# Local attention and FFT convolution on one core: filter spectrum and sine tables moved into batch 0's attention, crossbar transposes for batches 2 and 3, early casts by the DMA

## The chip, the cores and the metric

The kernel runs on one core of a Trainium2 chip. Times are device microseconds (us) of one execution, as a median over runs. The profile is one execution recorded by the hardware profiler. PE is TensorE (the matmul engine), DVE VectorE, ACT ScalarE, POOL GpSimd; SP only issues DMAs here. Each of PE, DVE, ACT and POOL has its own queue of instructions in the order of the program, and in the traces here one whose data is late holds up those behind it (experiment 4 has PE standing 4.3 us so). An eviction is the copy of a matmul's result out of PSUM. A crossbar transpose is a DMA that transposes on its way (`dma_start_transpose`). A run is called slow when it is over 1.5% above the fastest of the same kernel; ratios leave slow runs out.

## The reference

Four batches of 8-head attention (768 positions, head size 64), each query seeing 8 global keys and the 96 last keys with an ALiBi bias, followed by a gated FFT convolution ("Hyena") and an output projection:

```python
scores = scale * np.matmul(q, k.transpose(0, 1, 3, 2)) + bias      # bias = -slope[h] * dist
a = softmax(np.where(is_global | is_local, scores, -1e9))
x = np.matmul(a, v).transpose(0, 2, 1, 3).reshape(4, 768, 512)
proj = x @ w_proj
x1, x2, x3 = proj[..., :D], proj[..., D:2*D], proj[..., 2*D:]
H = np.fft.rfft(filter_fft, n=S, axis=0)
y = x1 * np.fft.irfft(np.fft.rfft(x2, n=S, axis=1) * H, n=S, axis=1) * x3
return y @ w_out
```

The kernel does the FFTs as matmuls with sine tables that it computes itself. "Filter stage" is everything that depends on `filter_fft` and the tables: angles, sines, the filter's spectrum (`h1`, `h2`), and the inverse tables (transposes of the forward ones). A "gate" is one block of the product `x1 * x3` with its two projections; it needs no FFT and no table.

## The kernel before

Python generators emit small chunks of work; `weave` merges several generators into the one order in which every engine gets its instructions. A stream `(gen, n, a, b)` spreads its n chunks evenly over the part a to b of a stretch. Nothing is reordered afterwards: the position in this order decides what an engine waits behind.

```python
def emit(self):
    ...
    self.weave((self.attention(*qkv, *x, first=cast), 33, 0, 1))     # attention of batch 0, alone
    self.load_more_weights()                                         # gate weights
    loads = [qkv, self.load_batch(1)]
    self.load_w_out()
    for b in range(self.B):
        streams = [(self.hyena(b, *x, early=(b == 0)), 30, 0, 1)]    # early: 8 gates ahead of the FFT
        nx = None
        if b == 0:
            streams.insert(0, (self.filter_stage(), 16, 0.0, 0.4))
        ...
        if b + 1 < self.B:
            nx = self.new_x()
            streams.insert(0, (self.attention(*loads[b + 1], *nx), 33,
                               0.4 if b == 0 else 0.0, 0.95))
        self.weave(*streams)
        x = nx

def filter_stage(self):                       # angles by PE and ACT, folded by DVE, sines by ACT
    self.fwd = self.cp.tile([P, 3, 6, P], F16)
    ths = []
    for a in range(4):
        ths.append(self.dft_angles(a))
        for k in range(2):
            self.after(k + 1, lambda k=k, a=a: self.dft_fold(k, *ths[a]))
        yield 1
    ...
    for a in range(4):
        self.dft_sines(a, ths[a][0])
    yield from self.filter_spectrum()
    yield from self.inverse_tables()

def transpose_q(self, hp, qt, first):         # q and k of each head pair are transposed by PE
    ...
    for st in range(6):
        nc.tensor.transpose(tq[:, P * st:P * st + P], src[:, st], self.ident)
    ... nc.vector.tensor_copy(QT, tq[:, 0:S])
```

The five stretches of the program, in time: attention of batch 0; Hyena 0 with the filter stage and attention 1; Hyena 1 with attention 2; Hyena 2 with attention 3; Hyena 3.

The softmax here doesn't subtract the row's maximum and nothing guards it: scores larger than these inputs give would overflow.

Of the kernel before, what the change touches and what calls it, by code (L numbers as in the profile page):

```python
# [23 lines left out]
X1_SCALE = 64.0  # L24

# [19 lines left out]
class Fused:  # L45
# [45 lines left out]
    def batch_tiles(self):  # L91
        D = self.D
        qt = self.ld.tile([P, 6, self.H, D], F16, tag="q")
        kt = self.ld.tile([P, 7, self.H, D], F16, tag="k")
        vt = self.ld.tile([P, 7, self.H, D + 1], F16, tag="v")
        self.nc.gpsimd.memset(vt[:, :, :, D:D + 1], 1.0)  # L96
        return qt, kt, vt

    def load_tiles(self, dst, src, b):

        g, D = self.nc.gpsimd, self.D
        for t in range(7):
            lo = max(0, self.K0[t] - NG)
            hi = self.K0[t] + KL
            g.dma_start(dst[P - (hi - lo):P, t, :, 0:D],  # L105
                        src[b, :, lo:hi, :].rearrange("h p d -> p h d"))
            if t == 0:
                g.dma_start(dst[0:NG, 0, :, 0:D],
                            src[b, :, 0:NG, :].rearrange("h p d -> p h d"))
        if b > 0:  # L110
            self.nc.sync.dma_start(dst[0:NG, 1:7], dst[0:NG, 0:1].to_broadcast(
                [NG, 6] + list(dst.shape[2:])))

    def load_batch(self, b):
        g = self.nc.gpsimd
        qt, kt, vt = self.batch_tiles()
        for t in range(6):
            g.dma_start(qt[:, t], self.q[b, :, P * t:P * t + P, :].rearrange("h p d -> p h d"))  # L118
        self.load_tiles(kt, self.k, b)
        self.load_tiles(vt, self.v, b)  # L120
        return qt, kt, vt

    def load_first(self):


        nc, D = self.nc, self.D
        self.first = []
        for hp in range(4):
            hs = slice(2 * hp, 2 * hp + 2)
            for eng, src in ((nc.sync, self.q), (nc.sync, self.k)):  # L130
                st = self.stage([P, 2, 6, D])
                eng.dma_start(st.rearrange("p h r d -> p h (r d)"),
                              src[0, hs].rearrange("h (p r) d -> p h (r d)", r=6))
                self.first.append(st)

    def cast_first(self, hp):
        sq, sk = self.first[2 * hp:2 * hp + 2]
        out = []
        pool = self.nc.gpsimd.tensor_copy
        for cp, src in ((pool if hp > 1 else self.nc.vector.tensor_copy, sq),  # L140
                        (pool if hp > 1 else self.nc.scalar.copy, sk)):
            t = self.mp.tile([P, 6, P], F16, tag=f"c{len(out)}", name="t")
            cp(t.rearrange("p t (h d) -> p t h d", h=2), src.rearrange("p h t d -> p t h d"))
# [3 lines left out]
    def stage(self, shape):  # L147
        t = self.mp.tile([P, 768], F32, tag="stg", bufs=6)
# [8 lines left out]
    def load_weights(self):  # L157
        g, cp, DM = self.nc.gpsimd, self.cp, self.DM
        self.w = cp.tile([P, 4, 3 * DM], F16)
        self.wr = self.w_proj.rearrange("(t p) n -> p t n", p=P)  # L160
        g.dma_start(self.w[:, :, DM:2 * DM], self.wr[:, :, DM:2 * DM])
        self.fl = self.mp.tile([P, 6, DM], F16, tag="g", bufs=2)
        g.dma_start(self.fl, self.filt.rearrange("(t p) n -> p t n", p=P))

    def load_more_weights(self):
        for o in (0, 2 * self.DM):
            self.nc.gpsimd.dma_start(self.w[:, :, o:o + self.DM], self.wr[:, :, o:o + self.DM])
# [6 lines left out]
    def distances(self):  # L174
# [4 lines left out]
        for ap, w, first in ((dg, n, NG), (dm[:, 2, n - 48:n], 48, NG + o)):  # L179
            g.iota(ap, pattern=[[1, w]], base=first, channel_multiplier=-1,  # L180
                   allow_small_or_imprecise_dtypes=True)

            for sgn, off in ((1, 0), (-1, NL - 1)):
                if w == 48 and sgn < 0:
                    continue
                g.affine_select(ap, ap, pattern=[[sgn, w]], base=off + sgn * first,
                                channel_multiplier=-sgn, compare_op=Alu.is_ge, fill=HUGE)

        g.affine_select(dm[:, 2, n - 48:n], dm[:, 2, n - 48:n], pattern=[[0, 48]],
                        base=-NG - o, channel_multiplier=1, compare_op=Alu.is_ge, fill=HUGE)  # L190
# [3 lines left out]
        v.memset(dm[0:NG, :, 0:KL], float(NL))  # L194
        v.memset(dm[0:NG, :, KL:n], HUGE)
        v.memset(dm[0:NG, 2, n - 48:n], float(NL))
        d0 = dm[0:NG, 0, 0:KL]
        v.memset(d0, HUGE)
        for sgn, off in ((1, 0), (-1, NL - 1)):
            g.affine_select(d0, d0, pattern=[[sgn, KL]], base=off, channel_multiplier=-sgn,  # L200
                            compare_op=Alu.is_ge, fill=float(NL))
# [8 lines left out]
    def dft_rows(self):  # L210

        nc, sp = self.nc, self.sp
        i = self.mp.tile([1, 384], I32, tag="p2", name="i")
# [10 lines left out]
    def dft_angles(self, a):  # L224
# [26 lines left out]
        nc.scalar.activation(th, an, Act.Copy, bias=MAGIC, scale=1.0 / S)  # L251
        return th, an

    def dft_fold(self, k, th, an):
        if k == 0:
            self.nc.vector.tensor_scalar(th, th, MAGIC, -float(self.S), op0=Alu.subtract,
                                         op1=Alu.mult)
        else:
            self.nc.vector.tensor_add(th, th, an)
# [9 lines left out]
    def busy(self, n):  # L269


        if n:
            pt = self.mm()
# [3 lines left out]
    def inverse_tables(self):  # L277
# [3 lines left out]
        for sp in range(3):  # L281
            tp = self.ps.tile([P, 1024], F16, tag="tr", bufs=1)
# [4 lines left out]
            nc.vector.tensor_copy(self.inv[:, 2 * sp:2 * sp + 2].rearrange("p c r -> p (c r)"),  # L287
# [39 lines left out]
    def filter_stage(self):  # L327
        self.fwd = self.cp.tile([P, 3, 6, P], F16)
        ths = []
        for a in range(4):  # L330
            ths.append(self.dft_angles(a))
            for k in range(2):
                self.after(k + 1, lambda k=k, a=a: self.dft_fold(k, *ths[a]))
            yield 1
        yield 1
        yield 1
        for a in range(4):
            self.dft_sines(a, ths[a][0])
# [3 lines left out]
    def filter_spectrum(self):  # L342
# [4 lines left out]
        f2 = [self.mp.tile([P, 3, DM], F16, tag="stg", bufs=6, name="f2") for _ in range(2)]  # L347
# [5 lines left out]
        sc = 2.0 * H_SCALE  # L353

        def evac(s, pt):
            if s < 4 and s % 2 == 0:
                nc.scalar.mul(self.h1[:, s], pt, sc)
                nc.vector.tensor_scalar(self.h1[:, s + 1], pt, sc, None, op0=Alu.mult)
                if s == 0:
                    nc.scalar.mul(self.h1[0:1, 0], pt[0:1], H_SCALE)  # L360
            elif s < 4:
                nc.scalar.mul(self.h2[:, s - 1], pt, sc)
                nc.vector.tensor_scalar(self.h2[:, s], pt, -sc, None, op0=Alu.mult)
                if s == 1:
                    nc.scalar.mul(self.h1[0:1, 1], pt[0:1], H_SCALE)
                    nc.vector.memset(self.h2[0:1, 0:2, :], 0.0)
            else:
                nc.scalar.mul(self.h1[0:64, s], pt[0:64], sc)
                nc.scalar.mul(self.h1[64:P, s], pt[0:64], sc)
                nc.vector.tensor_scalar(self.h2[0:64, s], pt[64:P], sc, None, op0=Alu.mult)  # L370
                nc.vector.tensor_scalar(self.h2[64:P, s], pt[64:P], -sc, None, op0=Alu.mult)
        for s in range(6):
            self.forward(s, f2[0], f2[1], evac)
            yield 1


    def attention(self, qt, kt, vt, xT, xa, xb, first=None):
# [3 lines left out]
        qk, cst = {}, {}  # L381

        def trq(i):
            if i < n:
                qk.setdefault(i, {})[0] = self.transpose_q(i, cst[i][0] if first else qt, first)

        def trk(i):
            if i < n:
                qk.setdefault(i, {})[1] = self.transpose_k(i, cst[i][1] if first else kt, first)

        def sc(i, g):
            if i < n:
                self.weights(i, g, qk[i][0], qk[i][1])
                if first and g > 0 and i + 1 < n:
# [9 lines left out]
        def trx(i):  # L404
            self.transpose_x(i, xn.pop(i), xT)
# [9 lines left out]
        if first:  # L415
            cst[0] = first
        trq(0)
        yield 1
        cast(1)
        trk(0)  # L420
        yield 1
        for i in range(n + 1):
            if first and i == 1:
                self.nc.vector.tensor_copy(vt[0:NG, 1:7], vt[0:NG, 0:1].to_broadcast(
                    [NG, 6, self.H, self.D + 1]))
            for live, fn in ((i < n, lambda: sc(i, 0)),
                             (i + 2 < n and first, lambda: cast(i + 2)),
                             (i + 1 < n, lambda: trk(i + 1)),
                             (i < n, lambda: sc(i, 1)),
                             (i > 0, lambda: val(i - 1, 0)),  # L430
                             (i + 1 < n, lambda: trq(i + 1)),
                             (i > 0, lambda: val(i - 1, 1)),
                             (i < n, lambda: sc(i, 2)),
                             (i > 0, lambda: trx(i - 1))):
# [10 lines left out]

    def transpose_q(self, hp, qt, first):
        nc, S = self.nc, self.S
        hs = slice(2 * hp, 2 * hp + 2)
        QT = self.ap_.tile([P, S], F16, tag="qT")
        tq = self.ps.tile([P, 1024], F16, tag="tr", bufs=1)  # L450
        src = qt if first else qt[:, :, hs, :]
# [299 lines left out]
```

## Time and profile before

The prediction was made from 239.95 us (median of 3 runs).

| stretch | us | PE busy | ACT busy | DVE busy | granted clock |
|---|---|---|---|---|---|
| attention 0 | 45.2 | 31.4 | 21.8 | 30.3 | 0.89 |
| Hyena 0, filter, attention 1 | 73.4 | 56.8 | 43.6 | 50.0 | 0.88 |
| Hyena 1, attention 2 | 43.9 | 41.8 | 30.1 | 33.1 | 1.00 |
| Hyena 2, attention 3 | 43.9 | 41.7 | 30.0 | 33.1 | 1.00 |
| Hyena 3 | 34.2 | 28.9 | 18.9 | 14.7 | 1.00 |

It comes from the busy time by windows of the kernel before. Columns: window, its length, then busy us (and count of instructions) of PE, PE's weight loads, DVE, ACT and POOL, granted PE clock, DMA share and GB/s (the DMA share is the time of all packets over that of the 16 engines, and can pass 1):

```profile
0.00:45.20 45.20, 31.36 (x279) 16.96 (x280) 30.27 (x70) 21.78 (x29) 35.83 (x55) 0.89 2.01 191
45.20:118.60 73.40, 56.84 (x447) 30.28 (x446) 49.98 (x95) 43.57 (x69) 27.30 (x35) 0.88 1.10 65
118.60:162.50 43.90, 41.82 (x400) 23.54 (x398) 33.09 (x71) 30.10 (x51) 12.06 (x14) 1.00 1.27 100
162.50:206.40 43.90, 41.65 (x394) 23.29 (x392) 33.08 (x71) 30.04 (x50) 0.00 (x0) 1.00 0.10 37
206.40:240.60 34.20, 28.88 (x154) 14.71 (x152) 14.69 (x27) 18.94 (x35) 0.00 (x0) 1.00 0.18 67
```

Two steady stretches are 95% full on PE; the second stretch is 77% full, at a lower clock, and is the long one. The page's rows of busy tenths in 40 slices (6 us each, counted from 0) of the kernel before show where:

```profile
PE   4575968887978665867999999899999997999883
PEclk9998597997999995697999999999999999999999
DMA  6999999999991000002999910033000002400006
```

The DMA engines are full (9 tenths, by the packets' time) until slice 12 (72 us), and PE has its holes in slices 13 to 18 (78 to 114 us). The chain of waits of the kernel before (start, duration, what) shows what the second stretch waits for first:

```profile
53.07 1.28 ACT L267
54.36 2.40 ACT fwd L267 x4
...
57.24 0.51 ACT h_767 L357
57.77 0.70 DVE h_767 L358
58.49 0.59 ACT h_767 L360
59.08 0.49 ACT h_768 L362
59.59 0.70 DVE h_768 L363
60.31 0.59 ACT h_767 L365
```

L267 are the table load for Sin and the sines, L357 to L365 the filter's evictions, alternating between ACT and DVE. And one oddity of attention 0, from its timeline on DVE and on POOL:

```profile
15.46 3.52 DVE L506 TENSOR_TENSOR E_96<-E_96,mask 128x432 f16<-128x432 f16 x2
16.36 3.30 POOL L143 CAST t<-t 128x768 f16<-128x768 f32 x4
```

Two DVE multiplies that take 0.38 us each elsewhere (median of 32) took 3.52 us together while POOL casted.

### The profile page before, as it was taken

The numbers are of one execution on the slowest core, as the hardware profiler recorded it, in microseconds if no ns is written. First come the engines' busy times: TensorE is split into PE (matmuls) and PEld (weight loads), VectorE is DVE, ScalarE is ACT, GpSimd is POOL, SyncE is SP. The second block draws the span as 40 slices with busy tenths as digits, with TensorE's granted clock in tenths as the row PEclk, the third lists the DMA queues.
The fourth block names the chain that finished last, engine by engine and source line by source line (L and its number), as shares of the span: only waits on it lengthen the run. The fifth ranks groups of instructions, "written<-read, shape, count | busy, mean of one in ns | idle before, by whom it ended". The sixth has DMA issues, their size and how long they took to land.

```text
span 240.6 us, 4274 instructions
## 1 busy us (share of the span) xinstructions
PE 200.6 (83%) x1664; PEld 108.8 (45%) x1664; DVE 161.1 (67%) x334; ACT 144.4 (60%) x232; POOL 75.2 (31%) x102
## 2 busy tenths in 40 slices
PE   4575968887978665867999999899999997999883
PEld 1333545332445342544545565455556554455541
DVE  5587586683675896597246999943599994139550
ACT  4462574477553863573668748466866765774643
POOL 6969478987930000004977200000000000000000
PEclk9998597997999995697999999999999999999999
DMA  6999999999991000002999910033000002400006
GB/s 190 347 132 197 204 155 149 122 171 148 129 119 11 0 3 0 3 0 18 191 246 142 114 10 3 0 143 123 0 3 0 4 0 102 162 0 0 3 34 229
DMA packets 79572, 21.68 MB, mean 90 GB/s; under 512 B 71328, under 2 KB 76480, under 8 KB 79552
## 3 DMA queue, kind: packets, MB, share of 16 engines
q0 software_dynamic: 73584, 11.67, 86.1%
q1 hardware_dynamic: 5968, 9.74, 12.2%
q8 instruction: 13, 0.21, 0.4%
q14 instruction: 7, 0.06, 0.1%
HBM read 26.48 MB, written 6.29 MB: 136 GB/s over the span
## 4 chain that ended last, share of the span: by engine, by line
PE 47%; DVE 23%; ACT 10%; issue 3%; ACTq 0%; DVEq 0%
PE pt L552 9%; PE pt L566 9%; PE pt L649 8%; PE pt L631 5%; PE pt L323 4%; DVE g L557 3%; DVE xn L527 3%; PE sp L490 3%; ACT E_99 L497 3%; PE tx L534 2%; PE o L517 2%; PE o L522 1%; PE tk L478 1%; PE tq L453 1%; DVE X L592 1%
## 5 line engine op out<-in xcount | busy, mean ns | idle before, releaser
L552 PE MATMUL pt<-xT,w 128*128 128x384 f16 x256 | 47.8, 331 | 2.1 <-ACT x_861 L556 1.7
L552 PEld LDWEIGHTS <-w 128*128 128x128 f16 x256 | 24.1, 99 | 18.8 <-issue 4.4
L497 ACT ACTIVATE E_99<-sp 128x864 f16<-128x864 f32 x24 | 21.5, 897 | 13.4 <-PE sp L490 12.7
L649 PE MATMUL pt<-wo,y 128*128 128x512 f16 x96 | 24.4, 396 | 2.6 <-DVE y L642 2.6
L497 ACT ACTIVATE E_96<-sp 128x864 f16<-128x864 f32 x24 | 21.5, 894 | 7.7 <-PE sp L490 7.6
L105 POOL DMA_DIRECT2D vt<-in_v_dram x28 | 25.1, 911 | 2.6 <-DMA kt<-in_k_dram 1.2
L490 PE MATMUL sp<-QT,KT 64*128 64x216 f16 (+2 forms) x224 | 18.5, 258 | 6.4 <-ACT E_99 L497 2.6
L631 PE MATMUL pt<-inv,X 128*128 128x384 f16 x96 | 20.6, 351 | 3.7 <-DVE X L592 3.6
L652 ACT ACTIVATE t<-pt 128x512 f32<-128x512 f32 x24 | 14.3, 597 | 13.7 <-PE pt L649 13.6
L105 POOL DMA_DIRECT2D kt<-in_k_dram x21 | 18.9, 916 | 6.8 <-DMA qt<-in_q_dram 3.3
L527 DVE TENSOR_TENSOR xn<-o,rc 128x448 f16<-128x448 f32 x32 | 20.0, 625 | 1.1
L568 ACT CAST dst<-pt 128x512 f16<-128x512 f32 x24 | 14.1, 587 | 8.8 <-PE pt L566 8.8
L323 PE MATMUL pt<-dst,fwd 128*128 128x512 f16 x72 | 18.9, 380 | 0.0
L275 PE MATMUL pt<-idle 128*128 128x512 f16 x38 | 17.7, 503 | 1.2 <-DVE idle L674 1.2
L535 ACT COPY xT<-tx 128x768 f16<-128x768 f16 x16 | 12.8, 798 | 8.5 <-PE tx L534 8.4
L490 PEld LDWEIGHTS <-KT 64*128 64x128 f16 x224 | 7.8, 96 | 21.9 <-issue 18.6
L595 ACT CAST X<-pt 128x512 f16<-128x512 f32 x24 | 14.1, 587 | 4.9 <-PE pt L323 4.6
L534 PE MATMUL tx<-ident,xn 128*128 128x128 f16 x112 | 9.8, 232 | 8.1 <-DVE xn L527 8.1
L118 POOL DMA_DIRECT2D qt<-in_q_dram x18 | 15.9, 904 | 0.2 <-issue 0.2
L96 POOL MEMSET vt<- 128x56 f16 x4 | 1.6, 412 | 43.3 <-PE o L522 43.3
L649 PEld LDWEIGHTS <-y 128*128 128x128 f16 x96 | 9.1, 102 | 13.2 <-DVE y L642 4.0
L631 PEld LDWEIGHTS <-X 128*128 128x128 f16 x96 | 8.9, 103 | 11.1 <-DVE X L592 4.7
(231 smaller groups left out, 393.5 us busy)
## 6 DMA issues: line engine op xcount, KB each, us to landing
out_dram<-t SPq DMA_DIRECT2D x24, 256.0 KB, 2.6
vt<-in_v_dram POOLq DMA_DIRECT2D x24, 128.0 KB, 7.0
qt<-in_q_dram POOLq DMA_DIRECT2D x18, 128.0 KB, 8.2
kt<-in_k_dram POOLq DMA_DIRECT2D x18, 128.0 KB, 6.5
t<-in_q_dram SPq DMA_DIRECT2D x4, 384.0 KB, 6.1
t<-in_k_dram SPq DMA_DIRECT2D x4, 384.0 KB, 7.1
w<-in_moe_w_proj_dram POOLq DMA_DIRECT2D x3, 512.0 KB, 9.7
fl<-in_moe_filter_fft_dram POOLq DMA_DIRECT2D x1, 768.0 KB, 10.4
```

What stands on the lines that cost most here:

```text
L105: g.dma_start(dst[P - (hi - lo):P, t, :, 0:D], src[b, :, lo:hi, :].rearrange("h p d -> p h d"))
L118: g.dma_start(qt[:, t], self.q[b, :, P * t:P * t + P, :].rearrange("h p d -> p h d"))
L275: self.nc.tensor.matmul(pt, self.idle[:, 0:P], self.idle, start=True, stop=True)
L323: self.nc.tensor.matmul(pt, self.fwd[:, kt, s, :], src[:, kt, :], start=(kt == 0), stop=(kt == 2))
L490: nc.tensor.matmul(sp[:, hh, off:off + w], KT[64 * hh:64 * hh + 64, o:o + P], QT[64 * hh:64 * hh + 64, KL * m:KL * m + w], start=(off == 0 ...
L497: nc.scalar.activation(eo, sp[:, :, 0:432].rearrange("p h (m w) -> p h m w", m=2), Act.Exp, scale=self.scale)
L527: nc.vector.tensor_mul(xn[:, :, hh, :], o[:, :, 0:D], rc.to_broadcast([P, 7, D]))
L534: nc.tensor.transpose(tx[:, KL * t:KL * t + P], xn[:, t, :, :], self.ident)
L552: nc.tensor.matmul(pt[:, 0:h], self.w[:, c, o + P * j:o + P * j + P], xT[:, c, h * s:h * s + h], start=(c == 0), stop=(c == 3))
L566: nc.tensor.matmul(pt, src[:, c, P * t:P * t + P], self.w[:, c, DM:2 * DM], start=(c == 0), stop=(c == 3))
L631: nc.tensor.matmul(pt[:, 0:h], X[:, s, cs], self.inv[:, s, :], start=(s == slots[0]), stop=(s == slots[-1]))
L649: nc.tensor.matmul(pt, y[:, c, P * t:P * t + P], self.wo[:, c, :], start=(c == 0), stop=(c == 3))
```

## The change

Its intent: let attention 1 run beside the whole of Hyena 0, by having filter and tables ready; take the q and k transposes of batches 2 and 3 off PE; relieve POOL and DVE early on. The core of the diff:

```diff
+LATE = 26
+GATES = (1, 0, 0, 0, 1, 0, 3)              # gates spread among the FFT chunks
...
     def load_batch(self, b):
+        def transposed():
+            self.nc.sync.dma_start_transpose(KT.rearrange("c t a p -> c (t a) p"),
+                                             kt.rearrange("p t h d -> p (t h d)"))
+            for t in range(6):
+                self.nc.sync.dma_start_transpose(QT[:, :, t],
+                                                 qt[:, t].rearrange("p h d -> p (h d)"))
+        vt = self.batch_tiles()
+        if b > 1:
+            self.after(LATE, transposed)
+        self.load_tiles(vt, self.v, b)
+        if b == 1:                          # gate weights now behind k, q, v of batch 1
+            for part in (0, 2):
+                self.load_w_in(part)
+            self.load_w_out()
...
-                               0.4 if b == 0 else 0.0, 0.95))
+            streams.insert(0, (self.attention(*loads[b + 1], *nx, natural=b == 0),
+                               34 if b == 0 else 25, 0.0, 0.9))
...
+        ths = [self.dft_angles(a) for a in range(4)]      # ahead of the first queries
+        for a in range(4):
+            if a == 2:
+                cast = self.cast_first(0)
+            self.dft_fold(*ths[a])
+        for a in range(2):
+            self.dft_sines(a, ths[a][0])
+        self.load_pairs((1,), nc.gpsimd, F16)             # the DMA casts
+        self.load_tiles(vt, self.v, 0)
+        self.load_pairs((2, 3), nc.gpsimd, F16)
...
-        self.weave((self.attention(*qkv, *x, first=cast), 33, 0, 1))
+        self.weave((self.attention(None, None, vt, *x, first=(cast, ths)), 34, 0, 1),
+                   (self.filter_stage(), 10, 0.7, 1))
```

Cut from it: a fold of the angles in one DVE operation instead of two (with one more ACT pass), shorter filter evictions, q evictions moved from DVE to ACT, transposes of batch 0 in the three-buffer PSUM pool, transposes of x one head pair later, `k` loaded ahead of `q`, first rows of k and v copied as soon as they land, output staging with 4 buffers instead of 6, and the use of `GATES`, by which Hyena 0 no longer has eight gates ahead of its FFT.

## The prediction

> **What bounds the kernel now.** By stretches of the trace (busy time by windows): attention of batch 0 takes 0 to 45.2 us (PE busy 31.4, part of it idle-weight matmuls, ACT 21.8, DVE 30.3, granted clock 0.89); batch 0's filter stage, Hyena and batch 1's attention 73.4 us (PE 56.8, clock 0.88); the two steady stages 43.9 us each with PE busy 41.8 and 41.7 at clock 1.00; the last Hyena 34.2 us with PE 28.9. So PE limits the steady stages, not the second stretch: its chain of waits runs 53.1 to 68.3 us almost only over ACT and DVE (table load 1.28, sines 2.40, then h1/h2 evictions of 0.59 and 0.70 in turns), and batch 1's attention starts only at about 75 us with too little Hyena work beside it (75 to 108 us: PE 23.4 of 33).
>
> **What the change does.**
> 1. Filter stage moves into batch 0's attention. Batch 1's attention then overlaps Hyena 0 from the start, a third steady stage that keeps its PE transposes. 73.4 becomes about 45 us (43.9 for the same work, plus 1 for q evictions on ACT and for loads). Saves about 28.
> 2. Batches 2 and 3 lose 24 q and 28 k transposes on PE and 4.7 us of DVE copies each. In the PE timeline of 119 to 162 us, seven k transposes hold PE 0.39 us and six q transposes 0.33, so 4 x 0.72 = 2.9 us per stage. 43.9 becomes 41 twice. Saves about 6.
> 3. Batch 0's attention pays. Before the first exp ACT gets four angle evictions of 0.6 to 0.8 and four rounding passes (about 5 us), four sines (2.4), a q eviction (0.95) and a table load (1.28): the first exp moves from 10.9 to about 12.3 us. Later ACT gets h1/h2 (5), inverse tables (2.4) and q evictions (2.9): about 30 us of ACT and 29 of DVE inside a 35 us loop, so 2 to 4 us longer. Given back: the DVE multiply that took 2.65 us instead of 0.38 beside POOL's casts (15.5 to 19.0 us), and the 1.9 us wait for the v copy. Net 45.2 becomes about 48; pair 2's load lands at about 20 us by my estimate, a little late.
> 4. The last stage is unchanged, 34.
>
> Sum: 48 + 45 + 41 + 41 + 34 = 209.
>
> **Crossbar transposes.** k and q of a batch are 0.92 and 0.79 MB. The Trainium skill, "DMA: Bandwidth & Descriptors", section "Latency and other measured facts", gives 261 GB/s for a transposing DMA; from it I estimate 7 us per batch. No trace here shows it. For batch 2 I expect input about 68 us and need at 93; for batch 3 about 97 and 134. So up to 25 us each stays hidden; beyond that PE waits.
>
> **Predicted** 209 us, 202 to 220; faster 0.95, same 0.03, slower 0.02.
>
> **What the after-profile would show.** Right: PE busy over 40 us in a stretch of about 45 after batch 0's attention, clock near 1.00; steady stages near 41 us with PE still above 90%; first exp about 12 us; batch 0's attention ending at 46 to 51 us with ACT and DVE about 60 to 70% busy.
>
> **What would make it wrong.** Slow crossbar transposes; output stores waiting behind them on SP; w0/w2 or v1 landing after 60 us (the DMA row is at 0.9 until 72 us); batch 0's attention growing over 52 us.

## The result

The changed kernel took 209.85 us (208.11 to 211.63, 4 runs, of which 211.63 counts as slow) against 240.91 us. Ratios here are the mean time of one kernel's fast runs over that of the other's fast runs of the same rounds, so they are not quite the ratio of the medians: 0.8702, 95% interval 0.86 to 0.8804.

| stretch | before | predicted | after | PE busy after |
|---|---|---|---|---|
| attention 0 (after: and filter) | 45.2 | 48 | 48.4 | 37.6 |
| Hyena 0, attention 1 | 73.4 | 45 | 45.7 | 42.8 |
| Hyena 1, attention 2 | 43.9 | 41 | 40.2 | 37.7 |
| Hyena 2, attention 3 | 43.9 | 41 | 40.0 | 38.4 |
| Hyena 3 | 34.2 | 34 | 34.2 | 28.9 |

Busy time by windows of the changed kernel, columns as above:

```profile
0.00:48.40 48.40, 37.64 (x333) 19.83 (x333) 32.58 (x89) 37.81 (x55) 40.66 (x61) 1.00 2.05 145
48.40:94.10 45.70, 42.84 (x396) 23.39 (x396) 32.33 (x69) 31.90 (x53) 28.95 (x34) 1.00 1.91 154
94.10:134.30 40.20, 37.72 (x339) 20.34 (x338) 29.35 (x63) 29.66 (x51) 8.16 (x10) 1.00 1.60 142
134.30:174.30 40.00, 38.38 (x341) 20.74 (x340) 29.35 (x63) 29.38 (x50) 0.00 (x0) 1.00 0.10 38
174.30:208.50 34.20, 28.92 (x155) 14.72 (x152) 14.68 (x27) 18.91 (x35) 0.00 (x0) 1.00 0.18 68
```

The second stretch now looks like the steady ones: PE 94% busy, at a clock of 1.00 instead of 0.88. No run separates what the clock alone is worth. The changed kernel's rows of busy tenths (slices of 5.2 us):

```profile
PE   7477997959999989987989999999899999998982
PEclk9999999999999999999999999999999999999999
DMA  4999999999999998999999940610000016000025
```

After attention 0 no long hole is left, the clock stays up, and the DMA engines are full through slice 22 (to about 120 us): the crossbar transposes and the loads of batch 3 run at the time at which the kernel before had PE's holes and idle DMA engines. The chain of waits of the changed kernel names two places where data, not an engine, comes last:

```profile
7.50 4.41 DMA vt<-in_v_dram
...
13.87 5.68 DMA t<-in_q_dram
19.58 0.37 DVE QT L164
...
87.47 0.61 ACT t L685
88.09 5.93 DMA out_dram<-t
94.13 0.60 ACT t L685
```

Attention 0 is held until 19.6 us by the queries of head pair 2, queued on POOL behind v. At 90.6 us ACT has no free staging buffer for Hyena 0's output, because stores have not landed; it stands idle for 2.9 us in two waits. What SP did just before (start, duration, instruction of the DMA queue):

```profile
70.63 7.63 SPq L127 DMA_TRANSPOSE KT<-kt  x1
78.36 8.93 SPq L130 DMA_TRANSPOSE QT<-qt  x6
87.38 7.70 SPq L686 DMA_DIRECT2D out_dram<-t  x6
```

The crossbar transposes of one batch hold SP for 16.7 us. The last should land at about 90 us (an estimate: issued at about 86.1 us, and the transposes of q whose landing the trace has took 3.6 to 4.1 us); PE computes batch 2's first scores at 91.6 us. The first store was issued at 87.38 us, 0.2 us after ACT had its tile ready (87.21), so SP's queue held it up by no more than that.

### The profile page after: what moved, and what is told of

Read it like the earlier page. It is cut to its first block, busy times and chain, and to the rows that moved or that the text cites. A ratio compares the mean times of both kernels' runs of the same rounds, so it can differ in the third digit from the quotient of the medians.

```text
span 208.5 us, 4047 instructions
## 1 busy us (share of the span) xinstructions
PE 185.5 (89%) x1557; PEld 99.0 (47%) x1557; DVE 138.3 (66%) x310; ACT 147.7 (71%) x242; POOL 77.8 (37%) x104
## 4 chain that ended last, share of the span: by engine, by line
PE 48%; DVE 21%; ACT 12%; DMA 8%; issue 5%; POOL 3%; POOLq 0%; ACTq 0%; DVEq 0%
PE pt L584 12%; PE pt L682 8%; PE pt L598 7%; PE pt L347 6%; ACT E L528 5%; PE sp L521 4%; DVE g L589 4%; PE pt L664 3%; DVE xn L559 3%; DMA out_dram<-t 3%; DMA t<-in_q_dram 3%; PE tr L566 3%; DMA vt<-in_v_dram 2%; PE o L549 2%; PE o L554 2%
## 5 line engine op out<-in xcount | busy, mean ns | idle before, releaser
L528 ACT ACTIVATE E<-sp 128x864 f16<-128x864 f32 x48 | 43.2, 900 | 7.2 <-PE sp L521 5.8
L540 DVE TENSOR_TENSOR E<-E,mask 128x864 f16<-128x864 f16 x32 | 19.1, 604 | 19.8 <-ACT E L528 16.5
L589 DVE TENSOR_TENSOR g<-pt,x 128x384 f16<-128x384 f32 x32 | 17.7, 554 | 11.4 <-PE pt L584 11.1
L682 PE MATMUL pt<-wo,y 128*128 128x512 f16 x96 | 22.4, 379 | 1.2 <-DVE y L675 1.2
L107 POOL DMA_DIRECT2D kt<-in_k_dram x21 | 18.9, 906 | 11.1 <-DMA w<-in_moe_w_proj_dram 4.9
L588 ACT ACTIVATE x<-pt 128x384 f16<-128x384 f32 x32 | 15.8, 494 | 8.8 <-PE pt L584 7.7
L664 PE MATMUL pt<-inv,X 128*128 128x384 f16 x96 | 18.3, 327 | 1.0 <-DVE X L628 0.9
L549 PEld LDWEIGHTS <-E 128*128 128x128 f16 x224 | 16.1, 99 | 4.9 <-issue 0.9
L549 PE MATMUL o<-vt,E 128*128 128x65 f16 x224 | 17.4, 196 | 0.0
L299 PE MATMUL pt<-idle 128*128 128x512 f16 x35 | 16.2, 470 | 1.3 <-DVE warm L709 1.2
L554 PE MATMUL o<-vt,E 128*128 128x65 f16 x192 | 16.3, 195 | 0.0
L567 ACT COPY xT<-tr 128x768 f16<-128x768 f16 x16 | 12.9, 803 | 3.6 <-PE tr L566 3.4
```

Source lines behind the costliest of these rows:

```text
L107: g.dma_start(dst[NG:P, t, :, 0:D], src[b, :, lo:lo + KL, :].rearrange("h p d -> p h d"))
L528: nc.scalar.activation(eo, sp[:, :, 0:432].rearrange("p h (m w) -> p h m w", m=2), Act.Exp, scale=self.scale)
L540: nc.vector.tensor_mul(eo, eo, mk[:, :, 0:2] if gi == 0 else mk[:, :, 1:3])
L549: nc.tensor.matmul(o[:, t, :], ef[:, c:c + P], vt[:, t, 2 * hp + hh, :], start=(t == 0), stop=(t == 0), skip_group_check=True)
L554: nc.tensor.matmul(o[:, t, :], ef[:, c:c + P], vt[:, t - 1, 2 * hp + hh, :], start=False, stop=True, skip_group_check=True)
L589: nc.vector.tensor_mul(g[:, j, h * s:h * s + h], p3[:, 0:h], x1)
```

## The experiments

The total was predicted well, so the question is whether the parts were. Twelve runs were made, one of them the changed kernel again; all were correct against the reference, and each ratio is to the kernel before in the same rounds. Stretches are counted from the first Hyena matmul of each batch.

### 1. The crossbar undone

```diff
-        return (QT, KT, vt) if b > 1 else (qt, kt, vt)
+        return qt, kt, vt                          # and no transposing DMA
-    ... natural=b == 0), 34 if b == 0 else 25,
+    ... natural=True), 34,
```

> The changed kernel with the crossbar undone: batches 2 and 3 get their q and k transposed by PE again, as batch 1 does. Theory (the PE time of the transposes, 2.9 us per steady stage, was on the limiting engine): stages of batches 1 and 2 go from 40.2 and 40.0 us back to 43 to 44, and the 6 us wait of batch 0's output stores behind the crossbar transposes at 88 us goes, which gives 2 to 3 us back in the stage before; total 213 to 216 us. Rival (the steady stages got shorter through the new order of gates and attention chunks, not through the crossbar): these stages stay at or under 41 us and the total is 209 us or less.

Measured: 216.64 us, ratio 0.8993 against 0.8702 with the crossbar; 2.9% of the kernel before, 7.0 us, and 0.6 us past the theory's edge. Its stretches by windows:

```profile
48.60:92.50 43.90, 41.99 (x398) 23.32 (x396) 32.48 (x69) 32.37 (x54) 34.98 (x42) 1.00 1.98 145
92.50:136.70 44.20, 41.99 (x399) 23.41 (x397) 31.45 (x67) 32.63 (x55) 1.50 (x2) 1.00 0.38 63
136.70:180.10 43.40, 41.56 (x391) 23.04 (x389) 31.44 (x67) 32.39 (x54) 0.00 (x0) 1.00 0.10 34
```

The theory holds for the steady stretches: the last of these, 43.4 us, is 40.0 us with the crossbar, and PE's busy time in it falls from 41.56 to 38.38. The rival falls. But the stretches of Hyena 0 and Hyena 1 together are 88.1 us without the crossbar and 85.9 with it: there it saves 2.2 us (2.7 with the control of experiment 3) and not 3.4 or more, so it gives something back, about 1 us. A likely place is ACT's wait for a staging buffer: 2.9 us of idling with the crossbar, 0.95 us before the same two evictions without it. The time from issue to landing of Hyena 0's stores (the trace has it for three of the six), first of the kernel with PE transposes, then of the changed kernel:

```profile
DMA to landing us min/median/max: 2.2/3.9/6.5
```

```profile
DMA to landing us min/median/max: 5.9/7.4/7.6
```

### 2. Is it SP's queue that delays the stores?

```diff
         if b > 1:
-            self.after(LATE, transposed)
+            transposed()                           # ahead of the row copy of v on SP
```

> The changed kernel with the crossbar transposes of a batch put on SP ahead of that batch's v row copy, so that they start when k and q have landed and not after v's first rows at 69.7 us. Theory (batch 0's output stores waited from 88 to 94 us only because SP was issuing transposes until 87.3 us): transposes end by 83 us, no wait of ACT for an output store, the two stages after 48 us take 83.5 to 84.5 us together instead of 86.3; total 2 to 3 us under the control. Rival (the wait at 88 us hides another limit just behind it, or earlier transposes collide with loads): within 1 us of the control.

Measured: 211.46 us, ratio 0.8753; the unchanged kernel 210.2 us, ratio 0.8722. The theory falls. The transposes were issued from 64.1 us and SP was free of them at 82.6 us, but the stores, issued from 89.0 us when ACT had the first of them ready, landed no earlier (the second at 95.9 us, against 94.0 in the changed kernel). Their time from issue to landing, known for four of the six:

```profile
DMA to landing us min/median/max: 5.6/5.8/6.8
```

The chain still had a 6.00 us wait for a store at 89.9 us. In this window batch 3's k and q are being loaded (POOL issues them from 81 to 97 us here, from 82 to 95 in the changed kernel, and from no earlier than the transposes of batch 2 let it: POOL waited 11.1 us for them). So it is not SP's queue that makes the stores late. What is left is the other traffic of the DMA engines. In the kernel without the crossbar these loads ran earlier, and the stores were faster. In the kernel before, which has no crossbar transposes at all, Hyena 0's stores took 5.4 us in the median while loads of a later batch ran (113.9 to 119.3 us), and the later stores of the changed kernel, with no loads beside them, took 2.0 to 2.1 us. That loads slow the stores is read from these coincidences, not tried by itself; nor is it shown how much transposes still in flight add, for k's transpose, issued 6.6 us earlier, landed only 1.6 us earlier (80.3 instead of 81.8 us). In the kernel before, with six staging buffers, ACT waited for none of those slow stores; whether six instead of four would do the same here was not tried.

### 3. The control

> The changed kernel unchanged, as the control of this call: 208 to 211 us, stages of 48, 44, 42, 40 and 34 us by the first Hyena matmul of each batch.

Measured: 210.2 us, ratio 0.8722 (0.8675 to 0.8768), stretches of 48.4, 44.0, 41.4, 39.9 and 34.3 us. It repeats the result.

### 4. The overlap alone, in the kernel before

```diff
-                                   0.4 if b == 0 else 0.0, 0.95))
+                                   0.0, 0.95))
```

> The kernel before with one number changed: batch 1's attention starts at 0.0 of the second stretch instead of 0.4. Theory (overlap is most of the gain): the second stretch falls from 73.4 to 57 to 62 us, although Exp and Sin tables are swapped twice more (2.6 us), total 224 to 230 us. Rival (the ACT and DVE chain of the filter, or batch 1's loads, bound that stretch): 235 us or more.

Measured: 254.18 us, ratio 1.0556. The theory falls: overlap alone, which is one half of the prediction's first step (the other moves the filter stage away), costs 13 us, and the second stretch grows from 73.4 to 85 us. From its chain of waits:

```profile
38.06 7.10 DMA kt<-in_k_dram
45.22 6.75 DMA kt<-kt
52.10 0.80 PE tk L478 x6
...
65.34 1.28 ACT L267
66.64 2.40 ACT fwd L267 x4
```

PE, in order, stands for 4.3 us, until 52.1 us, before k of batch 1, which was loaded late and whose first rows were copied to the other tiles only when all had landed. Then the sines stand in the chain again, with an Exp table load behind them. Late in the stretch (106 to 116 us) PE is busy for 5.2 of 10 us only, as in experiment 6, and the granted clock of the stretch fell from 0.88 to 0.80. How the 13 us divide among these was not taken apart.

### 5. The sines alone, in the kernel before

```diff
+        self.busy(2); self.dft_rows(); self.distances(); ...
+        ths = [self.dft_angles(a) for a in range(4)]
+        ...                                        # fold as in the changed kernel
+        for a in range(4):
+            self.dft_sines(a, ths[a][0])           # ahead of the first queries
-    streams.insert(0, (self.filter_stage(), 16, 0.0, 0.4))
+    streams.insert(0, (self.filter_stage(), 10, 0.0, 0.4))   # spectrum and inverse tables only
```

> The kernel before with only the angles and sines moved ahead of the first queries (with the changed kernel's fold). Theory (same as for n_sines_in_hyena0): batch 0's attention grows from 45 to 47 or 48 us, the second stretch shrinks from 73.4 to 62 to 65 us, total 231 to 235 us. Rival (the second stretch is bound by the late start of attention 1 and by loads): 238 us or more.

Measured: 234.56 us, ratio 0.9663. The theory's total holds: 8.1 us of 241.25. Its profile fell in a slow run, so its stretches are not used. But experiments 6 and 7 have the same early sines, and there attention 0 took 45.2 and 45.5 us against 45.2 in the kernel before: the 47 or 48 us of the theory did not come.

### 6. Sines, overlap and load order together, in the kernel before

```diff
# to experiment 5:
-                                   0.4 if b == 0 else 0.0, 0.95))
+                                   0.0, 0.95))
-        self.load_more_weights()
         loads = [qkv, self.load_batch(1)]          # k ahead of q, first rows copied at once
+        self.load_more_weights()
```

> k_before_sines_early plus batch 1's attention starting with Hyena 0, plus the changed kernel's load order (k, q, v of batch 1 ahead of the two gate weights, first rows copied at once), because c_before_overlap waited until 52 us for k of batch 1. Theory (sines early, loads in the order of use and overlap together are the gain; overlap alone cost 13 us): the second stretch falls to 50 to 54 us, total 220 to 226 us. Rival (something else is needed: gate order, shorter filter evictions, filter in attention 0): 230 us or more.

Measured: 231.97 us, ratio 0.9559, second stretch 61.9 us. The theory falls again, and the rival, that something else is needed, holds: overlap with its data in time is worth at most another 1% beside the sines, and that is not clear of the noise (fast runs of 230.6, 230.5 and 233.4 us here, of 235.8, 233.3 and 232.9 us in experiment 5). Its window of 78 to 90 us:

```profile
78.00:90.00 12.00, 6.20 (x67) 3.23 (x66) 11.20 (x24) 5.76 (x9) 0.00 (x0) 0.84 0.00 0
```

DVE is 93% busy, with the products of the FFT and with attention, and PE 52%: all eight gates of Hyena 0 had been computed early, so nothing is left that PE could do meanwhile.

### 7. The gates spread out

```diff
-            streams = [(self.hyena(b, *x, early=(b == 0)), 30, 0, 1)]
+            streams = [(self.hyena(b, *x, early=False), 30, 0, 1)]
```

> l_before_sines_overlap_loads (232.0 us) with the eight early gates of Hyena 0 spread over the later chunks, as the other batches have them; they had stood early only because the tables came late. In l, PE was busy 3 to 6 tenths from 80 to 101 us, behind DVE work on products, with no gate matmuls left to fill in. Theory (those gates are the missing filler): the second stretch goes from 61.9 to 52 to 56 us, total 221 to 226 us. Rival (the DVE chain itself bounds it, fillers or not): 229 us or more.

Measured: 226.48 us, ratio 0.9381, second stretch 56.6 us: just past the theory's edge, 226, and well under the rival's 229. The same window:

```profile
78.00:90.00 12.00, 11.62 (x120) 7.10 (x119) 11.48 (x24) 8.30 (x16) 0.00 (x0) 1.00 0.01 1
```

DVE is as busy as before, but PE now is 97% busy beside it. The matmuls of the gates are the filler.

### 8. From the other end: the filter stage put back

```diff
-        self.weave((self.attention(...), 34, 0, 1), (self.filter_stage(), 10, 0.7, 1))
+        self.weave((self.attention(...), 34, 0, 1))
+            if b == 0:
+                streams.insert(0, (self.filter_stage(), 10, 0.0, 0.4))
-                                   0.0, 0.9))
+                                   0.4 if b == 0 else 0.0, 0.9))
```

> The changed kernel with the filter stage (sine tables still early) put back beside Hyena 0, and batch 1's attention started at 0.4 of that stage, as before the change. Theory (the gain of 28 us is overlap of batch 1's attention with all of Hyena 0): batch 0's attention shrinks from 48.4 to about 44 us, the stage after it grows from 45.7 to 62 to 68 us, total 224 to 232 us. Rival (the gain came mostly from the table load and sines no longer standing in the chain at 53 to 57 us): total at or under 216 us.

Measured: 219.66 us, ratio 0.9118, attention 0 42.5 us, second stretch 61.0 us. Neither theory is right: it is between them. It is not quite a clean measure of overlap either, for with attention 1 out of the way Hyena 0 reached its first gate so soon that PE waited 1.0 us, until 53.7 us, for the gate weights.

The same with attention 1 started at once (only the last two lines of the diff left out):

> As b_filter_late, but batch 1's attention starts with Hyena 0 at once. Theory (where the filter stands matters little, when the attention starts matters much): batch 0's attention about 44 us, the next stage 51 to 54 us, total 211 to 215 us. Rival (the filter has to hide behind batch 0's attention): close to b_filter_late, 222 us or more.

Measured: 212.74 us, ratio 0.8815. The theory's total holds: when attention 1 starts is worth 3.0% (with the wait for weights in it), where the filter stands 1.1% (2.7 us) at most. The latter is not clear of the noise: the intervals, 0.8734 to 0.8896 and 0.86 to 0.8804, overlap. Its profile fell in a slow run and is not used.

### 9. The sines elsewhere

The filter stage as in experiment 8, with the angles and sines in it, and so with the eight early gates:

```diff
# to b_filter_late:
-        ths = [self.dft_angles(a) for a in range(4)]       # and folds and sines, ahead of the queries
     def filter_stage(self):
+        for a in range(4):
+            ths.append(self.dft_angles(a)); self.after(1, ...dft_fold...); yield 1
+        ...
+        for a in range(4):
+            self.dft_sines(a, ths[a][0])
-    hyena(b, *x, early=0)
+    hyena(b, *x, early=8 * (b == 0))
```

> b_filter_late (219.7 us) with the angles and sines in that stage too, and the eight early gates that the kernel before has there. Theory (the part of the gain that b_filter_late did not take away, some 14 us beside the crossbar, is the sine chain leaving the second stretch): batch 0's attention ends at about 41 us, the next stage grows from 61 to 68 to 72 us, total 225 to 231 us. Rival (that part comes from load order, casts and evictions): 218 to 222 us.

Measured: 231.73 us, ratio 0.958: 4.6% of the kernel before more than b_filter_late, just past the theory's edge; sines and gate order are both in it. What matters most is attention 0, first of this kernel, without the sines, then of b_filter_late, with them:

```profile
0.00:42.40 42.40, 27.15 (x276) 14.84 (x276) 25.31 (x76) 22.67 (x30) 35.51 (x54) 0.92 1.79 149
```

```profile
0.00:42.50 42.50, 32.17 (x290) 17.17 (x291) 27.65 (x80) 30.45 (x43) 35.70 (x54) 1.00 1.70 149
```

Ahead of the first queries, 7.8 us of ACT work cost 0.1 us, though the first exp came at 12.7 us instead of 9.3. In the kernel before it is the same: with early sines (experiment 6) the first exp came at 15.3 us instead of 10.9, and attention 0 still took 45.2 us. One reserve: the granted clock rose with the early sines (0.92 to 1.00 here, 0.89 to 1.00 there), and what that gave back is not separated. Now the sines inside attention 0, from 0.52 of it on:

```diff
-                   (self.filter_stage(), 10, 0.7, 1))
+                   (self.filter_stage(), 16, 0.52, 1))    # with the angles and sines in it
```

> The changed kernel with angles and sines moved from ahead of the first queries into the filter stage, which now starts at 0.52 of batch 0's attention (two more table swaps of 1.28 us between Exp and Sin there). Theory (early sines fill time in which ACT has nothing else to do): the first exp comes at about 9.5 instead of 12.7 us, but batch 0's attention ends 2 to 5 us later than 48 us; total 211 to 215 us. Rival (it does not matter where in batch 0's attention they stand): 208 to 211 us.

Measured: 220.33 us, ratio 0.9116, against 0.8722 for the control: 9.5 us lost, twice what the theory allowed; attention 0 ended at 59.8 us. The first exp came at 9.3 us as expected, but this gained nothing. From ACT's timeline:

```profile
9.26 0.89 ACT L535 ACTIVATE E<-sp 128x864 f16<-128x864 f32 x1 [1.81 <-PE sp L528]
...
21.70 0.80 ACT L494 COPY KT<-tr 128x768 f16<-128x768 f16 x1 [5.80 <-PE tr L492]
```

ACT ran ahead and then stood idle for 5.80 us until the queries of pair 2 had landed at 20.4 us, where the changed kernel is too. So much of the time ahead of 20 us is free for ACT, and here the 7.8 us moved out of it, with two more table loads of 1.28 us, cost about their own length later. The granted clock of attention 0 fell to 0.86 as well (1.00 in the changed kernel); its share was not separated.

### 10. Data first: the casts by the DMA undone

```diff
-        self.load_pairs((0,), self.nc.sync, F32)
+        self.load_pairs((0, 1), self.nc.sync, F32)
-        self.load_pairs((1,), nc.gpsimd, F16)
+        self.load_pairs((2,), nc.sync, F32)
         self.load_tiles(vt, self.v, 0)
-        self.load_pairs((2, 3), nc.gpsimd, F16)
+        self.load_pairs((3,), nc.sync, F32)
# and experiment 2's edit
```

> f_transposes_first, and the cast by DMA undone: pairs 1 to 3 of batch 0 are loaded as f32 by SP, cast by DVE in the repacking copies (0.67 instead of 0.3 to 0.5 us each), which frees POOL's queue for v. Theory (batch 0's attention is held until 20 us by pair 2, queued on POOL behind eight loads of v, which is also why early sines cost nothing): pair 2 is repacked before 14 us, the new limit is v at 18 to 19 us, batch 0's attention ends at 45 to 46.5 us; total 4 to 5 us under the control. Rival (ACT and DVE work bounds batch 0's attention, not data): it ends within 0.7 us of f_transposes_first or later.

Measured: 211.91 us, ratio 0.8754, the same as experiment 2 alone (0.8753). Attention 0 ended at 48.1 us, against 48.4 in the control and not the 45 to 46.5 of the theory. The theory falls in a telling way. From DVE's timeline, then from the chain of waits:

```profile
10.58 1.37 DVE L164 CAST QT<-t 128x768 f16<-128x768 f32 x2
```

```profile
5.92 5.67 POOL vt L107 x6
11.58 11.27 DMA vt<-in_v_dram
```

Pair 2 was repacked at 10.6 us instead of 19.6, and v, issued earlier than in the changed kernel, landed at 22.9 us. All these loads share the DMA engines; taking one out of the queue makes another the last. So data holds attention 0 until 20 to 23 us in either order, and who casts made no difference to the time. The rival is not excluded for the rest: in the changed kernel, after 21 us of attention 0 only POOL waits for a DMA, and the chain runs over PE, ACT and DVE.

## Why the prediction was right or wrong

The total and every stretch came out close: 209 predicted, 209.85 measured, no stretch off by more than 1 us. The steps behind the numbers fared less well.

- Step 2 (crossbar: "2.9 us per stage", "41 twice") was right in mechanism and a little small. Beside the same kernel with PE transposes, the last steady stretch fell by 3.4 us and PE's busy time in it by 3.2.
- Step 4 was right: 34.2 us both times.
- Step 1, "batch 1's attention then overlaps Hyena 0 from the start ... saves about 28", had the right end state, and 45 us followed from that alone; what it did not have is the share of each cause. It took the second stretch of the changed kernel for a steady one, which it is, and named two causes together, the filter stage out of the way and the overlap. The overlap by itself costs 13 us (experiment 4). Of the filter stage the early sines are worth 3.4% (5), the place of the rest at most about 1% (8). It did not name the gates as filler, worth 1.8% (7), nor the order of loads, which was changed together with the overlap (6) and not tried alone. Going up from the kernel before, in ratios of their own rounds:

| kernel | ratio | step |
|---|---|---|
| before | 1 | |
| sines early (5) | 0.9663 | -3.4% |
| and overlap, load order (6) | 0.9559 | -1.0% |
| and gates spread (7) | 0.9381 | -1.8% |
| the change without the crossbar (1) | 0.8993 | -3.9% |
| the change | 0.8702 | -2.9% |

  The table is one path; the parts depend on each other and would share differently in another order, and the step of 1.0% is not clear of the noise. Of the 3.9%, the filter's place in attention 0 is at most 1.1% by experiment 8; the rest (shorter filter evictions, q evictions on ACT, transposes in the larger PSUM pool, x transposed later) was not taken apart.
- Step 3, "batch 0's attention pays. Before the first exp ACT gets ...", had 48 us right, through a sum whose terms were not; that they cancelled is luck. The first exp came at 12.7 us (12.3 predicted), but the sum counted this delay, and it was not paid: the early sines cost 0.1 us, because the data holds attention 0 until about 20 us (experiments 9 and 10). Without sines and filter the changed kernel's attention 0 takes 42.4 us, so the other edits gave back 2.8 us. The payment was the filter stage, 5.9 us and not "2 to 4": 42.5 us without it (8), 48.4 with it. The "about 60 to 70% busy" held for DVE (67%) and not for ACT (37.81 of 48.4 us, 78%).
- Crossbar: "I estimate 7 us per batch" was mis-sized. From 70.6 to about 90 us it took 19; 1.70 MB in that time is 90 GB/s. The estimate took a bandwidth for the limit, but issuing them alone held SP for 16.7 us, and for batch 3 again 16.7 us, though from 116 to 122 us the DMA share was 0.82 and then 0.45. The sum was saved by the allowance made beside it, 25 us of slack, and narrowly: the transposes of batch 2 landed some 2 us ahead of use (91.6 us).
- Of what would make it wrong, "output stores waiting behind them on SP" came true by 1 to 2 us in its effect, but not in its cause: with SP free in time, the stores landed no earlier (experiment 2).
- "The DVE multiply that took 2.65 us": right. A pair of them in attention 0 of the changed kernel takes 0.67 us together, with no POOL cast beside it. The Trainium skill, "SBUF — State Buffer", section "Who interferes with whom", states that a VectorE instruction with two inputs in SBUF contends with a GpSimd instruction that reads SBUF. The multiply reads E and mask, both in SBUF, and the 3.52 us of the kernel before agree with it; no run tries this by itself.

## What to carry to other kernels

An ablation from one end does not give what a part is worth: an overlap that crowns a change can be a loss by itself, if the data comes late, if a serial chain of another engine stands in the same queue, or if the filler was used up early. Look for the time in which an engine can do nothing because data is on its way, and put preparatory work there: here it cost 0.1 us, and 9.5 us in the middle of the same stage. Before moving a load forward, ask which load it pushes back: in experiments 2 and 10, with the DMA engines full, another order changed which transfer came last, and not the time.

## What the Trainium skill lacked or had wrong

- "DMA: Bandwidth & Descriptors", section "Latency and other measured facts", gives 261 GB/s for a transposing DMA with a non-contiguous middle dimension (and more for a contiguous one), and "Advanced Engine Details and Errata", section "X-Bar Transpose (TRN2)", says that they are "as fast as regular DMAs". Here, from SBUF to SBUF, 1.70 MB took about 19 us (90 GB/s) beside other loads, and from 119 to 122 us, when the DMA share was down to 0.45, transposes still ran at 92 GB/s. The time that SP is held by issuing one is given only in cycles, for tiles of unstated size and "previous generations"; here it was 7.63 us for 28 blocks of 128x128 and 8.93 us for six DMAs of 4 blocks, where a plain store held it for 0.33 us.
- "ScalarE: Activation LUTs", section "What ACT_TABLE_LOAD costs", gives about 1.28 us and some 1.4 us of drain for a switch of tables. The 1.28 us are in the trace; the drain is not: between the eviction before the load at 53.07 us and the first sine at 54.36 us there was no more than that.
- No page read for this says how much slower a store gets beside casting loads: issue to landing of a 256 KB store was 2.0 to 2.1 us in the later stretches, and 5.9 to 7.6 us while batch 3 was loaded.
